# Ten late half modes fetched mode by mode, the mix-in one mode later, and the last 64 rows stored over three queues

## The chip, the cores and the metric

The kernel runs on one core of a Trainium2 chip. The metric is the device time of one execution in microseconds; each number given as "time" is a median over runs. A profile of one execution goes with it; its span runs from the first to the last instruction and is a little shorter than the time.

In this text PE or TensorE is the matrix engine, DVE or VectorE the vector engine, ACT or ScalarE the scalar engine, POOL or GpSimd the general engine, SP or sync the queue that only issues transfers. A q behind an engine's name means its instruction queue.

## The reference

Eight batches, eight heads, 576 positions, 64 channels per head. First a masked attention: heads 0 to 3 look at the last 32 positions, heads 4 to 7 at every 32nd position. The heads side by side are x (8 x 576 x 512). Then a spectral mix:

```python
X = np.fft.rfft(x, axis=1)
Y = np.zeros_like(X)
Xr, Xi = (np.real(X[:, :n_modes]), np.imag(X[:, :n_modes]))      # n_modes = 64
Yr = np.einsum('bmd,mde->bme', Xr, w_r) - np.einsum('bmd,mde->bme', Xi, w_i)
Yi = np.einsum('bmd,mde->bme', Xr, w_i) + np.einsum('bmd,mde->bme', Xi, w_r)
Y[:, :n_modes] = Yr + 1j * Yi
y = np.fft.irfft(Y, n=S, axis=1)
u = x + y
return (u + np.maximum(u @ w_ch, 0.0)).astype(np.float32)
```

Each of the 64 modes has a complex 512 x 512 matrix of its own, `w_r[m]` and `w_i[m]`, in 32-bit floats: 2 x 64 MB that have to be read once. All else is small beside it.

## The kernel before

**Weights.** A mode's matrix is split into two halves of 256 rows (a "half mode"); the list `ORDER` says in which sequence the 128 half modes are read. Its last 24 entries are half 1 of modes 56 to 63 and then half 0 of modes 48 to 63. `w_fetch` fetches two half modes, m and m + 1, into one tile `wt`: real parts on partitions 0 to 63, imaginary parts on 64 to 127. Normally that is one transfer for the real and one for the imaginary part of both modes, 512 KB each as 16-bit floats in the tile (the transfer converts). From entry 124 on (`i < 2 * NM - 4`), it is one transfer for each mode and part, 256 KB, sorted by mode: real and imaginary of m, then of m + 1. All are issued by GpSimd, in order. The tiles come from a pool of five (`NWBUF`), and a new fetch is asked for after the second mode of a pair has been multiplied.

**The order of the work.** The program is written out by hand, engine by engine in the order of the Python loops. While the weights stream in, the attention is computed, then its spectrum, then the modes are multiplied as they come: `mode(0, m)` for half 1 (pairs, line 597) and `mode(1, m)` for half 0 with m from 48 on (one mode at a time, line 630, 16 small products into one PSUM bank of eight modes). `spectrum` on VectorE (line 563) adds a group of modes to the tile `YT`. For the last group this is done twice: for modes 56 to 61 right after mode 61, and for modes 62 and 63 after mode 63.

**The late loop.** Its 24 steps are `rest`: steps 0 to 7 are half 1 of modes 56 to 63, steps 8 to 23 are half 0 of modes 48 to 63. Behind the products of step i come the functions in `late[i]`. Most are `renew(b, ts)`: it takes two tiles of 128 rows of batch b, adds what modes 0 to 47 contribute through the inverse transform to u @ w_ch (matmuls at lines 956 and 760, result copied by ScalarE) and to u (line 760, added by VectorE at line 961). `renew(b, (4,))` does it for the last 64 rows of two batches, a "half tile". At step 22 stand `v_early` (line 987) and `u_early` (line 992), which start the first two output items in PSUM.

**The tail.** After the last mode, `spec_z(3, 0)` (line 736) multiplies the last 16 modes of batches 0 to 3 by `w_ch`, and 18 output items follow: 16 of 2 batches x 128 rows, then two of 4 batches x 64 rows. For each, `new_rows` (line 1001) adds the last modes, `v_done` (line 1013, ScalarE) takes the positive part, and `u_done` (line 1020, VectorE) adds it to u and stores it: from the sync queue at line 1028 for the first 16 items, at line 1031 for the 64-row items, from the scalar queue for odd batches and from sync for even ones. The program closes at line 1108 with a drain on each engine and a barrier.

Of the kernel before, what the change touches and what calls it, by code (L numbers as in the profile page):

```python
# [19 lines left out]
NM = 64  # L20
# [36 lines left out]
def kernel(  # L57
# [10 lines left out]
    nc = tc.nc  # L68
# [17 lines left out]
    def psum(kind, half=False, pair=False):  # L86
        if pair:
            return pss[kind].tile([128, 2, 512], FP, tag=kind, name=kind)
        if half:
            return pss[kind].tile([128, 1024], F16, tag=kind, name=kind)  # L90
        return pss[kind].tile([128, 512], FP, tag=kind, name=kind)
# [65 lines left out]
    def w_fetch(n=1):  # L157
        for _ in range(n):
            i = len(w_tiles)
            if i >= 2 * NM:  # L160
                return
            half, m = ORDER[i]
            if i // 2 in GUEST:
                wt = big.tile([128, 2, 4, DM], F16, tag=GUEST[i // 2], name="wt")
            else:
                wt = pw.tile([128, 2, 4, DM], F16, tag="w", name="wt")
            single = []
            for ri, src in enumerate((moe_w_r, moe_w_i)):
                dst = wt[ds(64 * ri, 64)]
                rows = src[m : m + 2, ds(256 * half, 256), :].rearrange(  # L170
                    "m (p c) e -> p m (c e)", c=4
                )
                dst = dst.rearrange("p m c e -> p m (c e)")


                ones = range(2)
                if ri and not m:
                    ones = [1]
                elif i in UNEVEN and not ri:
                    a = 0  # L180
                    for n in UNEVEN[i]:
                        nc.gpsimd.dma_start(dst[a : a + n], rows[a : a + n])
                        a += n
                    continue
                elif i < 2 * NM - 4:
                    nc.gpsimd.dma_start(dst, rows)  # L186
                    continue
                single += [(j, ri, dst[:, j], rows[:, j]) for j in ones]
            for _, _, to, rows in sorted(single, key=lambda x: x[:2]):
                nc.gpsimd.dma_start(to, rows)  # L190
            w_tiles.extend((wt[:, 0], wt[:, 1]))
# [393 lines left out]
    def mode_pair(slot, m):  # L585
        half = 1 - slot
        if m % 4 == 0:
            ypt[slot] = psum("y")
        yp = ypt[slot]
        steps = [(c, mm) for c in range(4) for mm in (m, m + 1)]  # L590
        if m == 0:
            steps.sort(key=lambda x: x[1])
        for c, mm in steps:
            wt = w_tiles[ORDER.index((half, mm))]
            pr = ds(0, 128 if mm else 64)
            a = 32 * (mm % 4)
            nc.tensor.matmul(  # L597
                yp[ds(a, 32), :],
                Xh[half][pr, c].rearrange("p b r (h m) -> p (b r h) m", h=2)[
                    :, :, mm % 32  # L600
                ],
                wt[pr, XC[c], :],
                start=(c == 0),
                stop=(c == 3),
                tile_position=(0, a),
            )
        if slot or m // 2 not in GUEST:
            w_fetch()
        if m % 4:
            yr = big.tile([128, DM], F16, tag="yr", name="yr")  # L610
            act_copy(yr, yp)
            queued.append(lambda: four_turned(slot, m - 2, yr))

    def mode(slot, m):
# [22 lines left out]
        if m % 2:  # L637
            w_fetch()
# [131 lines left out]
    strided_tokens()  # L770
    load_str(2, 2)
    w_fetch()

    def str_front(b):
# [66 lines left out]
    for b in range(B):  # L841
# [12 lines left out]
        n = 0  # L854
        nm = NMODES[b]
        for mi in range(nm):
# [3 lines left out]
            n = upto  # L860
# [66 lines left out]
    n = 0  # L927
    for m in range(SPLIT0):
# [4 lines left out]
        n = upto  # L933
# [7 lines left out]
    def spec_late(mm, kept, eng):  # L941
        up = psum("p", pair=True)
        for bq in range(2):
            mm(2, bq, up[:, bq])
        for b in range(B):
            eng(kept[b][64:96], up[ds(32 * (b % 4), 32), b // 4])

    def renew(b, ts):
        n = len(ts)
        if n == 2:  # L950
            v0, xo = v0s[b][:, ts[0] : ts[0] + 2], xos[b][:, ts[0] : ts[0] + 2]
        else:
            v0, xo = v0h[b // 2].unsqueeze(1), xoh[b // 2].unsqueeze(1)
        vp, up = psum("p", pair=True), psum("p", pair=True)
        for j, t in enumerate(ts):
            nc.tensor.matmul(vp[:, j], idn, v0[:, j], start=True, stop=False)
            rows_of(b, t, vp[:, j], zzs, False)
        act_copy(v0, vp[:, 0:n])
        for j, t in enumerate(ts):
            rows_of(b, t, up[:, j], yys, True)  # L960
        nc.vector.tensor_tensor(out=xo, in0=up[:, 0:n], in1=xo, op=AluOp.add)  # L961
# [2 lines left out]
        spec_late(spec_y, yys, lambda o, i: nc.vector.tensor_copy(out=o, in_=i))  # L964

    late = {0: [lambda: spec_late(spec_z, zzs, act_copy)], 1: [spec_last]}
    for n, i in enumerate([3, 5, 7] + list(range(8, 21))):
        b, t = n // 2, n % 2 * 2
        late[i] = [lambda b=b, t=t: renew(b, (t, t + 1))]
        if n % 4 == 3:  # L970
            late.setdefault(i + (b == B - 1), []).append(lambda b=b: renew(b, (4,)))
# [5 lines left out]
    LAST = len(items) - 1  # L977
    vps, ups, rls, osbs = {}, {}, {}, {}

    def own(item, kept, half):  # L980
        bs, t = item
        return [kept[b][:, t] for b in bs] if t < 4 else [half[b // 2] for b in bs[::2]]

    def v_early(k):
        vps[k] = psum("p", pair=True)
        for j, r in enumerate(own(items[k], v0s, v0h)):
            nc.tensor.matmul(vps[k][:, j], idn, r, start=True, stop=False)  # L987

    def u_early(k):
        ups[k] = psum(("p", "u")[k % 2], pair=True)  # L990
        for j, r in enumerate(own(items[k], xos, xoh)):
            nc.tensor.matmul(ups[k][:, j], idn, r, start=True, stop=False)
# [12 lines left out]
    def pieces(k):  # L1005
        return [slice(0, 1), slice(1, 2)] if k == 0 else [slice(0, 2)]
# [8 lines left out]
    def u_done(k):  # L1015
        bs, t = items[k]
        up, rl = ups.pop(k), rls.pop(k)
        osb = pw.tile([128, 2, DM], FP, tag="w", name="osb")
        for j in pieces(k):
            nc.vector.tensor_tensor(  # L1020
                out=osb[:, j], in0=up[:, j], in1=rl[:, j], op=AluOp.add
            )
            if t < 4:
                rows = out[:, ds(128 * (t - t % 2), 256), :].rearrange(
                    "b (p i) e -> p b i e", i=2
                )
                own_b = slice(bs[0] + j.start, bs[0] + j.stop)
                nc.sync.dma_start(rows[:, own_b, t % 2], osb[:, j])
        if t == 4:
            for b in bs:  # L1030
                (nc.scalar if b % 2 else nc.sync).dma_start(
                    out[b, ds(512, 64), :], osb[ds(64 * (b % 2), 64), b // 2 % 2, :]
                )

    flush()
    rest = [(0, m) for m in range(SPLIT1, NM)] + [(1, m) for m in range(SPLIT0, NM)]
    late[22] = [lambda: v_early(0), lambda: v_early(1), lambda: u_early(0)]
    for i, (slot, m) in enumerate(rest):
        mode(slot, m)
        for w in late.get(i, ()):  # L1040
# [19 lines left out]
    for k in range(2):  # L1060
        if k:
            u_early(k)
        new_rows(k, ups[k], yys)
        u_done(k)
    for k in range(2, LAST + 2):
        if k == 8:
            held = psum("p", pair=True)[:, 0]
            spec_z(3, 1, held)
            act_copy(zzs[1], held)
        if k <= LAST:  # L1070
            v_early(k)
        if k > 2:
            u_early(k - 1)
        if k <= LAST:
            new_rows(k, vps[k], zzs)
        if k > 2:
            new_rows(k - 1, ups[k - 1], yys)
        if k <= LAST:
            v_done(k)
        if k > 2:  # L1080
            u_done(k - 1)
# [31 lines left out]
```

The softmax here doesn't subtract the row's maximum and nothing guards it: scores larger than these inputs give would overflow.

## Time and profile before

| what | value |
|---|---|
| time, median of 3 | 427.74 us (427.74 to 428.25) |
| span of the profile | 426.7 us |
| TensorE busy | 346.4 us (81%) |
| VectorE, ScalarE busy | 234.7 us (55%), 218.3 us (51%) |
| transfers on the GpSimd queue | 81.28 MB into the chip's memory, 96.2% of the 16 DMA engines' span |
| rate in slices 2 to 36 of the 40 equal slices of the span | 210 to 215 GB/s |
| stores of the last 64 rows | 4 from sync, 4 from scalar, 128 KB each, first issue 420.2 us, last 422.3 us |

The rate counts bytes as they arrive, and the weights arrive at half their size, so about twice as much is read from memory. Lines such as `PE L630` name an engine and a line of the kernel; `y<-X,wt` is what is written and what is read; `<-DMA wt...` behind a bracket says what ended the idle time before.

### The profile page before, as it was taken

Reading aid. Unit: us, or ns where it says so; the run is one execution under the profiler, and the core shown is the slowest. Engines: PE = TensorE matmul, PEld = TensorE weight load, DVE = VectorE, ACT = ScalarE, POOL = GpSimd, SP = SyncE. Lnnn points to the kernel's source line nnn. Section 1 sums busy time; section 2 is a strip of 40 time slices with the busy share of each in tenths; the row PEclk is TensorE's granted clock in tenths of the full one; section 3 lists DMA queues with packets and bytes.
Section 4 is the critical chain, followed back from the end, with each engine's and each line's share of the span. In section 5 each row is a group of like instructions: output and inputs, shape, how many; then the busy total and the mean of one; then the engine's idle time right before and its main releaser. Section 6 shows DMA issues by size and latency. Waiting matters only on the chain.

```text
span 426.7 us, 9768 instructions
## 1 busy us (share of the span) xinstructions
PE 346.4 (81%) x4167; PEld 208.2 (49%) x4167; DVE 234.7 (55%) x466; ACT 218.3 (51%) x390; POOL 110.7 (26%) x196
## 2 busy tenths in 40 slices
PE   2977878769999698889768788878788867889993
PEld 2866767554656365566433344435444423445330
DVE  3788778851355154356113246746676354655884
ACT  1687678643656356556642235423442444443872
POOL 8332333322423222222222322222232222210000
PEclk9999899967999689999995889989999979989997
DMA  8999999999999999999999999999999999995698
GB/s 150 210 212 212 213 213 213 211 211 211 214 213 213 213 213 215 212 214 215 210 214 211 213 214 213 210 213 215 212 213 214 213 213 214 214 212 105 244 355 287
DMA packets 30938, 91.62 MB, mean 215 GB/s; under 512 B 4464, under 2 KB 5232, under 8 KB 30896
## 3 DMA queue, kind: packets, MB, share of 16 engines
q0 software_dynamic: 25168, 81.28, 96.2%
q1 hardware_dynamic: 4976, 9.13, 5.9%
q10 hardware_dynamic: 752, 0.61, 0.5%
q8 instruction: 32, 0.52, 0.5%
q14 instruction: 10, 0.08, 0.0%
HBM read 162.83 MB, written 9.44 MB: 404 GB/s over the span
## 4 chain that ended last, share of the span: by engine, by line
DMA 47%; PE 29%; DVE 14%; ACT 5%; issue 3%; DVEq 0%; POOL 0%; ACTq 0%; POOLq 0%
DMA wt<-in_moe_w_i_dram 38%; DMA wt<-in_moe_w_r_dram 7%; PE y L597 5%; DVE xb L241 3%; DVE kz L283 3%; PE p L987 2%; ACT X L251 2%; PE sc L532 2%; PE tp L413 2%; PE sc L459 1%; PE p L1001 1%; PE y L532 1%; PE p L760 1%; DVE yy L752 1%; DVE rec L240 1%
## 5 line engine op out<-in xcount | busy, mean ns | idle before, releaser
L597 PE MATMUL y<-wt,X 128*32 128x512 f16 (+1 forms) x448 | 70.9, 430 | 20.1 <-DMA wt<-in_moe_w_i_dram 20.1
L186 POOL DMA_DIRECT2D wt<-in_moe_w_r_dram x59 | 34.7, 588 | 126.4 <-PE y L597 56.3
L186 POOL DMA_DIRECT2D wt<-in_moe_w_i_dram x60 | 35.4, 590 | 68.3 <-DMA wt<-in_moe_w_i_dram 44.4
L597 PEld LDWEIGHTS <-X 128*32 128x32 f16 (+1 forms) x448 | 28.1, 140 | 39.4 <-DMA wt<-in_moe_w_i_dram 18.6
L727 DVE COPY xo<-tp 128x512 f16<-128x512 f16 x32 | 22.1, 691 | 36.8 <-PE tp L725 36.8
L726 ACT ACTIVATE v<-sc 128x512 f16<-128x512 f32 x32 | 19.1, 597 | 44.2 <-PE sc L717 44.2
L717 PE MATMUL sc<-w_cp,xT 128*128 128x512 f16 x128 | 36.9, 410 | 1.9 <-DVE xT L690 1.9
L489 ACT ACTIVATE PL<-sc 128x480 f16<-128x480 f32 (+1 forms) x48 | 27.0, 578 | 21.3 <-PE sc L475 21.0
L241 DVE TENSOR_TENSOR xb<-av,rec 90x256 f16<-90x256 f32 (+2 forms) x80 | 36.0, 450 | 2.8
L240 DVE RECIPROCAL rec<-av 90x4 f32<-90x4 f32 (+2 forms) x80 | 14.6, 183 | 39.3 <-PE av L504 28.2
L251 ACT ACTIVATE yr<-y 128x512 f16<-128x512 f32 x28 | 16.7, 597 | 36.8 <-PE y L597 35.6
L961 DVE TENSOR_TENSOR xo<-p,xo 128x1024 f16<-128x1024 f32 x16 | 19.6, 1225 | 21.7 <-PE p L760 21.7
L420 DVE COPY qT<-tp 128x576 f16<-128x576 f16 x16 | 11.9, 752 | 34.7 <-PE tp L413 34.7
L251 ACT ACTIVATE v<-p 128x1024 f16<-128x1024 f32 x16 | 16.4, 1023 | 23.1 <-PE p L760 23.1
L378 ACT ACTIVATE PL<-sc 90x360 f16<-90x360 f32 (+1 forms) x48 | 22.7, 490 | 7.0 <-PE sc L371 6.4
L251 ACT ACTIVATE v<-tp 128x640 f16<-128x640 f16 (+1 forms) x24 | 19.0, 807 | 11.8 <-PE tp L447 9.3
L413 PE MATMUL tp<-cI_s,ring 64*64 64x64 f16 x864 | 22.4, 197 | 2.7 <-DVE qT L420 2.4
L459 PE MATMUL sc<-cMl_s,cI_s 128*128 128x480 f16 (+1 forms) x48 | 19.4, 405 | 4.5 <-ACT PL L489 2.9
L276 PE MATMUL tp<-cI_s,ring 72*128 72x72 f16 x256 | 15.4, 207 | 8.7 <-DMA ring<-in_v_dram 7.1
L413 PEld LDWEIGHTS <-ring 64*64 64x64 f16 x864 | 17.5, 110 | 9.4 <-issue 5.4
L251 ACT ACTIVATE kz<-tp 64x360 f16<-64x360 f16 (+1 forms) x32 | 18.9, 592 | 6.2 <-PE tp L413 5.2
L1013 ACT ACTIVATE rl<-p 128x1024 f32<-128x1024 f32 (+1 forms) x19 | 18.4, 979 | 5.7 <-PE p L1001 3.1
(142 smaller groups left out, 737.9 us busy)
## 6 DMA issues: line engine op xcount, KB each, us to landing
wt<-in_moe_w_i_dram POOLq DMA_DIRECT2D x60, 512.0 KB, 18.8
wt<-in_moe_w_r_dram POOLq DMA_DIRECT2D x59, 512.0 KB, 17.7
out_dram<-osb SPq DMA_DIRECT2D x15, 512.0 KB, 3.4
ring<-in_v_dram POOLq DMA_DIRECT2D x8, 288.0 KB, 13.4
ring<-in_q_dram POOLq DMA_DIRECT2D x8, 288.0 KB, 13.6
ring<-in_k_dram POOLq DMA_DIRECT2D x8, 288.0 KB, 13.1
ring<-in_v_dram POOLq DMA_DIRECT2D x3, 512.0 KB, 14.8
ring<-in_q_dram POOLq DMA_DIRECT2D x3, 512.0 KB, 14.8
```

The costliest lines, as they stand in the source:

```text
L186: nc.gpsimd.dma_start(dst, rows)
L241: nc.vector.tensor_tensor(out=dst, in0=val.rearrange("p h (q c) -> p h c q", c=4), in1=rec[0:n, 0:pieces] .to_broadcast((n, pieces, 64)) . ...
L251: nc.scalar.activation(out=out, in_=in_, func=ACTF.Copy)
L378: nc.scalar.activation(out=PS[0:n, ds(POFF[t], 4 * n)], in_=scp[0:n, 0 : 4 * n], func=ACTF.Exp, scale=SCALE,)
L413: nc.tensor.transpose(tp[ds(64 * hp, 64), ds(64 * i, 64)], qn[ds(64 * hp, 64), ds(64 * (9 * g + i), 64)], idn[ds(64 * hp, 64), ds(64 * hp, ...
L459: nc.tensor.matmul(scp[:, 0 : n * times].rearrange("p (h x) -> p h x", h=times), idn, mask_rows("cMl", n, times), start=True, stop=False,)
L489: nc.scalar.activation(out=dst, in_=src, func=ACTF.Exp, scale=SCALE)
L597: nc.tensor.matmul(yp[ds(a, 32), :], Xh[half][pr, c].rearrange("p b r (h m) -> p (b r h) m", h=2)[:, :, mm % 32], wt[pr, XC[c], :], start= ...
L717: nc.tensor.matmul(vp, xT[:, ch], w_chs["cp"][:, ch, :], start=(ch == 0), stop=(ch == 3),)
L726: nc.scalar.activation(out=v0, in_=vp, func=ACTF.Copy)
L727: nc.vector.tensor_copy(out=xo.rearrange("p (h q c) -> p h q c", h=2, c=4), in_=tp[:, 0:512].rearrange("p (h c q) -> p h q c", h=2, c=4),)
L961: nc.vector.tensor_tensor(out=xo, in0=up[:, 0:n], in1=xo, op=AluOp.add)
```

## The change

Three edits. Five more pairs of half modes (modes 50 to 59 of half 0) are fetched mode by mode, so that the first mode of a pair can be multiplied before the second has come. The mix-in `renew` stands one mode step later from the third on; `u_early` moves behind the last mode. And the stores of the last 64 rows are issued from three queues (sync, scalar, GpSimd) in place of two, to shorten the row of issues at the end.

```diff
-                elif i < 2 * NM - 4:
+                elif i < 2 * NM - 14:
                     nc.gpsimd.dma_start(dst, rows)
                     continue
                 single += [(j, ri, dst[:, j], rows[:, j]) for j in ones]
...
-    for n, i in enumerate([3, 5, 7] + list(range(8, 21))):
+    for n, i in enumerate([3, 5] + list(range(8, 22))):
         b, t = n // 2, n % 2 * 2
         late[i] = [lambda b=b, t=t: renew(b, (t, t + 1))]
...
         if t == 4:
+            q = [nc.sync, nc.scalar, nc.gpsimd, nc.scalar if k == LAST else nc.gpsimd]
             for b in bs:
-                (nc.scalar if b % 2 else nc.sync).dma_start(
+                q[b % 4].dma_start(
                     out[b, ds(512, 64), :], osb[ds(64 * (b % 2), 64), b // 2 % 2, :]
                 )
...
-    late[22] = [lambda: v_early(0), lambda: v_early(1), lambda: u_early(0)]
+    late[22] += [lambda: v_early(0), lambda: v_early(1)]
+    late[23] = [lambda: u_early(0)]
```

With it, `renew` of the last batch's second pair of tiles falls to step 21 (mode 61) and its half tile to step 22, ahead of the two `v_early`. Of the first 64-row item (batches 0 to 3) sync and scalar store one batch each and GpSimd two; of the last one (batches 4 to 7) sync stores one, scalar two and GpSimd one.

## The prediction

> **What bounds the kernel now.** I read the page's slices first, then the chain of waits, then each late weight transfer's issue and landing, then the order of the tensor engine's work around the end of the stream, and last the end of the program. The queues and the chain come from the page:
>
> ```profile
> q0 software_dynamic: 25168, 81.28, 96.2%
> ...
> DMA 47%; PE 29%; DVE 14%; ACT 5%; issue 3%; DVEq 0%; POOL 0%; ACTq 0%; POOLq 0%
> ```
>
> The queue filled by GpSimd keeps 16 DMA engines at work for 96% of the span: the weights are the bound, until they have landed. The chain in order of time shows the hand-over:
>
> ```profile
> 357.73 19.38 DMA wt<-in_moe_w_i_dram
> 377.10 0.14 issue
> 377.24 0.64 PE y L630 x16
> ...
> 389.94 0.56 DVE YT L563
> 390.50 0.04 issue
> 390.54 0.64 PE y L630 x16
> ...
> 393.33 1.05 PE zp L736 x4
> ...
> 419.83 1.44 DVEq L1108
> ```
>
> From 377.24 on the chain runs over TensorE alone, and from 393.33 (`spec_z` on the last spectrum) over the tail of output items. So two questions decide: how much earlier can 393.33 be, and how soon after the last addition is the program over.
>
> For the first, the view of the weight tile, one transfer at a time. The last one:
>
> ```profile
> L190 POOL DMA_DIRECT2D wt<-in_moe_w_i_dram x1: 515/515/515, 382.3 to 382.3; - x1
> ...
> DMA to landing us min/median/max: 9.6/9.6/9.6
> ```
>
> 382.31 + 9.6 = 391.9 is the landing of mode 63's imaginary half. The same view gives, for the single transfers before it, 383.3, 384.5, 385.7, 387.0, 388.2, 389.5 and 390.7: one every 1.23 us. The pairs land at 367.3 (modes 52/53), 372.2 (54/55), 377.1 (56/57) and 382.1 (58/59), so 2.45 us for each transfer of twice the size. Per byte they are equal. The timeline of TensorE beside that:
>
> ```profile
> 377.24 0.64 PE L630 MATMUL y<-X,wt 128*128 128x16 f16 x16 [1.24 <-DMA wt<-in_moe_w_i_dram]
> ...
> 390.54 0.64 PE L630 MATMUL y<-X,wt 128*128 128x16 f16 x16 [0.53 <-DVE YT L563]
> 391.01 1.02 PE L987 MATMUL p<-v,cI_s 128*128 128x512 f16 x4
> 391.87 0.59 PE L992 MATMUL p<-xo,cI_s 128*128 128x512 f16 x2
> 392.31 0.64 PE L630 MATMUL y<-X,wt 128*128 128x16 f16 x16
> 393.33 1.04 PE L736 MATMUL zp<-w_ch,YT 128*128 128x512 f16 x4 [0.39 <-DVE YT L563]
> ```
>
> Mode 63 starts at 392.31, only 0.4 us after its weights are there. That 0.4 us is all that any reordering of TensorE can win, unless the stream itself ends sooner.
>
> For the second, the view of the line where the program ends:
>
> ```profile
> L1108 SPq EVENT_SEMAPHORE  x11: 17/28/28, 422.7 to 426.6; - x11
> L1108 POOLq EVENT_SEMAPHORE  x4: 17/17/17, 425.9 to 426.6; - x4
> L1108 POOLq DRAIN  x3: 51/98/12676, 382.3 to 426.4; - x3
> ```
>
> GpSimd's first drain starts with its last DMA (382.3) and takes 12.68 us: to 394.98. Its descriptor work was over at 382.31 + 0.52 = 382.83, so the drain waited for the transfers, and ended 3.1 us after the last of them landed (391.9). Today nobody notices: GpSimd isn't needed again until the closing barrier at 425.9.
>
> **What the Trainium skill says.** "DMA: Bandwidth & Descriptors", section "Issuing engines are not separate DMA queues": transfers started from several engines share the same 16 DMA engines, and starting them on several only saves issue time. The trace agrees: in the stretches of 1 us from 421 to 424 the DMA share is already 0.94, 0.97 and 0.95. Same page, "Latency and other measured facts": the first byte of a transfer from GpSimd takes about 1 us, from sync or scalar about 0.6 us; no store here leaves from GpSimd, so the trace doesn't show it for one. "Perfetto Trace Analysis", "DMA Instruction — SWDGE (GPSIMD)": the profiled bar ends when the descriptors are written, not when data has moved; the 0.52 us bar against the landing after 9.6 us agrees. "TensorE: Matmul & The Clock Gate", Part 1: after an idle window of about 3.4 us the clock halves. The trace has it at 378 to 380 (granted 0.50; a 128x512 matmul every 0.43 us instead of 0.22). I found no page that says what a drain on GpSimd waits for.
>
> **The change, part by part.** *Single transfers for modes 50 to 59.* Five pairs of 2 x 512 KB become 20 of 256 KB, 10 more issues. Each is 0.52 us on GpSimd, which idles about 1.9 us before each late issue: hidden. In the trace eight transfers are open at a time (when mode 63's last is issued at 382.31, the one eight before it has just landed at 382.1). Eight singles are 8 x 1.23 = 9.8 us of stream. The last eight of today run on that depth already, still at 1.23 us each, so I expect no loss. The stream's end stays at 391.9, give or take 0.4. What changes is that the first mode of each pair may start 2.45 us earlier: landings every 2.45 us, 372.2 (55), 374.7 (56), 377.1, 379.6, 382.1, 384.5, 387.0 (61), 389.5 (62), 391.9 (63).
>
> *Mix-in one mode later.* A mode (0.49 us) with one `renew` (1.29 us) takes 1.78 us, as between 386.81 and 388.60 - less than the 2.45 us of its weights; with the half tile too, 2.97 us (370.39 - 367.42). From mode 48 at 357.58 TensorE falls behind at first. The `renew` at mode step 7 is gone, so it idles from about 354 to 357.6, and may run the next 3.4 us at half clock: some 1.7 us. It catches up by 0.67 us a mode and is level with the stream at mode 60 (384.6). Then: mode 61 at 387.1, done with its `renew` at 388.9; mode 62 at 389.6. Its spectrum of six modes on VectorE is queued ahead of the last big addition and done near 388.2, so the 0.53 us wait goes. After mode 62 come 0.49 + 1.18 (half tile of the last batches) + 0.86 (`v_early` twice) = 2.53 us, to 392.15: mode 63 starts there instead of at 392.31. `u_early(0)`, 0.43 us, now lies behind mode 63, in the 0.54 us in which TensorE waits for VectorE's last spectrum: hidden. Gain on this path: 0.16 us; bounds 0.4 (all the slack) and -0.4 (stream later, or half clock at the end).
>
> *The tail* from 393.3 to the last addition's end at 420.06 + 1.22 = 421.28 isn't touched: ends at 421.12.
>
> *Stores of the last 64 rows.* Now 4 issues on sync and 4 on scalar, 0.56 to 0.58 us each, the last at 422.3 landing 3.3 us later, at 425.6; then 1.1 us to the end. After: of the last item one store on sync, two on scalar, one on GpSimd. Scalar's second starts at about 421.8 and lands at 425.1: 0.5 us earlier on that side. The GpSimd store is issued at 421.2. From issue to landing I bound it below by the 3.3 us of the other queues and above by the first load of the trace from GpSimd, 5.0 us for twice the bytes; I take 3.7, so 424.9. What stands behind it on GpSimd is the drain, and the barrier waits for that. Its excess over the landing is 3.1 us in the only case this trace has, which I take: 428.0. Lower bound 0 (if a short drain sees its one transfer at once), upper 5 us. From GpSimd's first barrier event to the end is 426.7 - 425.9 = 0.8: span 428.8.
>
> Sum: 428.8 - 426.7 = +2.1 us; 427.74 + 2.1 = **429.8 us**.
>
> **The rivals.** *A: the drain costs nothing.* Then the end hangs on the scalar queue: 425.1 + 1.1 = 426.2, 0.5 us sooner, 427.2 us. For it: the page's chain never names GpSimd's drain, and one drain over eight queued loads need not price one after a single store. Against: 12.68 us can't be a drain's own cost when the two others took 0.10 and 0.05.
> *B: faster, because the stream ends sooner.* From 388 to 391.5 the DMA share falls from 0.86 to 0.08: some engines lag. If smaller transfers even them out, mode 63 could start up to 1.5 us earlier if its queue on TensorE is shortened as well, and with a free drain the time is about 426.2. Against: that tail already consists of single transfers, and TensorE has 2.5 us of work between modes 62 and 63.
> *C: a shallower queue starves the stream.* If 9.8 us in flight isn't enough for the lagging engine, the ten modes cost perhaps 0.1 us each: 1 us more, 430.8 with the drain. Against: today's last eight singles.
> *D: the drain is dearer,* 5 us: 431.7.
>
> **How the numbers follow.** Drain as computed 0.52, C 0.06, D 0.06, A 0.20, B 0.16. The first three are slower by over 0.2% (0.86 us): 0.64. A is within it: 0.20. B is faster: 0.16. The range reaches from just under A, 427.0, to D, 431.7; it leaves out B and the worst of D and C.
>
> **What would show it.** Right: GpSimd's long drain begins near 421.2 and ends after 427, about 3 us behind its last store, and the closing events follow it; mode 63 starts within 0.4 us of 392.15; single landings stay at 1.23 us; the last addition ends near 421. Wrong: the first closing event of GpSimd follows sync's last by 0.1 us as today, or the last weight lands more than 1 us off 391.9.

## The result, and the profile after

The changed kernel takes 432.17 us (median of 4 runs, 431.53 to 434.46) against 427.74 us: ratio 1.0108, 95% interval 1.0089 to 1.0128. The prediction had the direction and the cause, a drain on GpSimd at the end, but at 429.8 us less than half of the size, and the time lies 0.5 us above its range.

The page of the changed kernel, queues and chain:

```profile
q0 software_dynamic: 25472, 81.67, 95.9%
...
DMA 48%; PE 21%; DVE 4%; issue 2%; ACT 2%; POOL 1%; POOLq 0%; DVEq 0%; ACTq 0%
```

The weights still fill 96% of the span. POOL has come into the chain with 1%, a small share with much behind it. The chain's last pieces in order of time (start, length, what):

```profile
418.12 1.24 DVE osb L1020
419.36 0.28 issue
419.64 0.47 POOL out_dram L1032
...
420.75 0.55 POOLq L1110
```

The chain's last piece begins at 420.75 on GpSimd and is followed only to 421.3, in a span of 429.8 us. What comes next is in the view of the program's last line (here L1110; count, shortest, median and longest in ns, first and last start):

```profile
L1110 SPq EVENT_SEMAPHORE  x11: 17/28/28, 422.6 to 429.7; - x11
L1110 POOLq EVENT_SEMAPHORE  x4: 17/17/17, 429.0 to 429.7; - x4
L1110 POOLq DRAIN  x3: 51/97/8218, 420.8 to 429.5; - x3
...
L1110 SPq DRAIN  x3: 7/7/7, 426.0 to 429.2; - x3
```

The long drain of GpSimd now starts at 420.75 and takes 8.22 us, to 428.97. Sync is through with its waits at 426.0, as before at 425.8; GpSimd's first closing event comes at 429.0, when the drain is over. Three microseconds lie between. The last store from GpSimd, in the view of the store line:

```profile
L1032 POOL DMA_DIRECT2D out_dram<-osb x1: 529/529/529, 420.8 to 420.8; - x1
...
DMA to landing us min/median/max: 4.6/4.6/4.6
```

It landed at 420.76 + 4.6 = 425.4, so the drain outlasted it by 3.6 us.

And the end of the weight stream, in TensorE's timeline of the changed kernel:

```profile
356.77 0.64 PE L630 MATMUL y<-X,wt 128*128 128x16 f16 x16 [3.52 <-DMA wt<-in_moe_w_i_dram]
...
386.50 0.64 PE L630 MATMUL y<-X,wt 128*128 128x16 f16 x16 [0.51 <-DMA wt<-in_moe_w_i_dram]
...
389.21 0.64 PE L630 MATMUL y<-X,wt 128*128 128x16 f16 x16 [0.76 <-DMA wt<-in_moe_w_i_dram]
...
391.52 0.64 PE L630 MATMUL y<-X,wt 128*128 128x16 f16 x16
391.99 0.59 PE L992 MATMUL p<-xo,cI_s 128*128 128x512 f16 x2
392.54 1.04 PE L736 MATMUL zp<-w_ch,YT 128*128 128x512 f16 x4
```

The last weights land at 391.3 (issued 381.68, 9.6 us), and mode 63 starts at 391.52, 0.8 us sooner than in the profile of before. That looks like a gain and is none: mode 48, whose weights no edit touches, already starts at 356.77 against 357.58. From there to mode 63 it is 34.75 us now and 34.73 before; from mode 63 to the end of the last addition (420.49) it is 28.97 us in both. From mode 48 on the two profiles differ in one stretch alone: from the last addition to the end it is 9.3 us against 5.4.

### The profile page after: what moved, and what is told of

Read it like the earlier page. It is cut to its first block, busy times and chain, and to the rows that moved or that the text cites. A ratio compares the mean times of both kernels' runs of the same rounds, so it can differ in the third digit from the quotient of the medians.

```text
span 429.8 us, 9787 instructions
## 1 busy us (share of the span) xinstructions
PE 340.9 (79%) x4167; PEld 206.4 (48%) x4167; DVE 235.1 (55%) x466; ACT 218.3 (51%) x390; POOL 117.0 (27%) x209
## 4 chain that ended last, share of the span: by engine, by line
DMA 48%; PE 21%; DVE 4%; issue 2%; ACT 2%; POOL 1%; POOLq 0%; DVEq 0%; ACTq 0%
DMA wt<-in_moe_w_i_dram 31%; DMA wt<-in_moe_w_r_dram 13%; PE y L597 5%; DMA ring<-in_v_dram 4%; PE sc L717 3%; PE p L987 2%; PE p L1001 1%; DVE yy L752 1%; PE p L992 1%; PE y L532 1%; PE tp L725 1%; ACT X L251 1%; PE u L992 1%; PE tp L413 1%; PE sc L459 1%
## 5 line engine op out<-in xcount | busy, mean ns | idle before, releaser
L597 PE MATMUL y<-wt,X 128*32 128x512 f16 (+1 forms) x448 | 67.6, 413 | 22.5 <-DMA wt<-in_moe_w_i_dram 22.4
L186 POOL DMA_DIRECT2D wt<-in_moe_w_r_dram x54 | 31.8, 589 | 110.2 <-PE y L597 35.7
L186 POOL DMA_DIRECT2D wt<-in_moe_w_i_dram x55 | 32.6, 592 | 64.3 <-DMA wt<-in_moe_w_i_dram 40.1
```

What stands on the lines that cost most here:

```text
L597: nc.tensor.matmul(yp[ds(a, 32), :], Xh[half][pr, c].rearrange("p b r (h m) -> p (b r h) m", h=2)[:, :, mm % 32], wt[pr, XC[c], :], start= ...
```

## The experiments

The kernel before was timed again with each group of experiments, at 427.86 to 427.99 us, and each ratio below is against its own group.

**1. Stores back on two queues.**

```diff
-            q = [nc.sync, nc.scalar, nc.gpsimd, nc.scalar if k == LAST else nc.gpsimd]
-                q[b % 4].dma_start(
+                (nc.scalar if b % 2 else nc.sync).dma_start(
```

> The changed kernel with the stores of the last 64 rows on two queues as before; single transfers and the later mix-in stay. Theory S (the store edit costs everything; the other two edits are worth nothing): 427.7 us, within 0.5 of before, and from mode 48's start to mode 63's start 34.7 us as in both kernels. Rival W (the single transfers or the later mix-in cost part of it): 428.5 us or more. Rival G (they gain what the profile seems to show, the last addition 0.8 us earlier): 426.9.

428.32 us (13 runs), ratio 1.0013 (0.9998 to 1.0029). In the profile mode 48 starts at 356.72, mode 63 at 391.52, the last addition ends at 420.49 and the span at 426.0. The time alone, 0.46 us above before with an interval that takes in 1, would not settle rival W; but the median span of these runs is 426.2 us and that of before's 426.1, so within the span the other two edits neither gain nor cost. The store edit carries almost everything; rival G falls.

**2. The store edit alone,** on the kernel before (the same two lines as in the change).

> The kernel before with only the store edit. Theory S: 431.6 to 432.2 us; last addition to end 9.3 us against 5.4 before; GpSimd's drain ends 3 to 4 us after its last store has landed, and the closing events follow at once. Rival W: less than 430.5.

431.64 us, ratio 1.0085 (1.0070 to 1.0101). Last addition to end: 430.1 - 421.1 = 9.0 us. Its own drain, and GpSimd's closing event behind it:

```profile
L1109 POOLq EVENT_SEMAPHORE  x4: 17/17/17, 429.4 to 430.0; - x4
L1109 POOLq DRAIN  x3: 51/98/7976, 421.4 to 429.9; - x3
```

The long drain runs from 421.36 for 7.98 us, to 429.3, and the closing event follows at 429.4. The store edit alone makes 3.8 of the 4.4 us of loss.

**3. No GpSimd store in the last item.**

```diff
-            q = [nc.sync, nc.scalar, nc.gpsimd, nc.scalar if k == LAST else nc.gpsimd]
+            q = [nc.sync, nc.scalar] * 2 if k == LAST else [nc.sync, nc.scalar, nc.gpsimd, nc.gpsimd]
```

> The changed kernel with GpSimd storing only batches 2 and 3 of the first 64-row item; the last item on sync and scalar. Theory S with a drain of landing plus a fixed excess of 3.1 to 3.6 us: GpSimd's last store is issued 0.57 us sooner and so the end comes about 0.6 to 1.0 us sooner, 431.2 us. Rival N (the excess grows with the number of open transfers, 3 then and 2 now): 1.5 us or more sooner, 430.5. Rival L (only a store behind the last addition matters): 427.7.

The profile ends 1.0 us sooner (428.8; median span of the runs 429.0 against 429.95), the drain at 420.11 + 7.90 = 428.01, 3.5 us behind its last landing (420.2 + 4.3). That is theory S with the same excess for two transfers as for three. The time is 431.74 us, ratio 1.0090 (1.0069 to 1.0110), hardly below the changed kernel's: two of four runs have 0.8 to 1.6 us more outside the span than the usual 1.8 (see the last section). Rival L falls in any case.

**4. One early store from GpSimd,** on the kernel before.

```diff
-                nc.sync.dma_start(rows[:, own_b, t % 2], osb[:, j])
+                (nc.gpsimd if k == 8 else nc.sync).dma_start(rows[:, own_b, t % 2], osb[:, j])
```

> The kernel before with one 512 KB store, that of item 8, some 11 us ahead of the last addition, issued from GpSimd. Theory S with a drain of landing plus 3.1 to 3.6 us: the drain is over long before the end, 427.7 us, and its end minus the landing gives the excess for a single transfer, 3.1 to 3.6 us. Rival F (any store from GpSimd has a fixed price at the end): 429 us or more. Rival N (excess grows with open transfers): same time, but an excess near 1 us.

428.33 us, ratio 1.0014 (1.0006 to 1.0022): 0.5 us, not 4. The drain, in the view of its last line:

```profile
L1108 POOLq DRAIN  x3: 51/98/6885, 408.5 to 425.9; - x3
```

It ends at 408.5 + 6.9 = 415.4, long before the end, and 3.6 us behind the landing of its one transfer (408.52 + 3.3 = 411.8). So neither a store from GpSimd as such nor the number of open transfers sets the price of 4 us: rivals F and N fall. The trace has the other 0.5 us elsewhere. Up to the store's issue the DMA share matches that of before, microsecond by microsecond; then, between 409 and 410, it is 0.40, where the stretches of 1 us on either side and the one of before at this place have 1.02 to 1.04: the engines ran dry for some 0.6 us before this store's bytes moved. Until the last addition they stay near 1, so the gap isn't made up: from the last addition to the end it is 5.9 us in place of 5.4.

**5. One GpSimd store in all,** that of batch 6 in the last item.

```diff
-            q = [nc.sync, nc.scalar, nc.gpsimd, nc.scalar if k == LAST else nc.gpsimd]
+            q = [nc.sync, nc.scalar, nc.gpsimd if k == LAST else nc.sync, nc.scalar]
```

> The changed kernel with one GpSimd store only, of batch 6 in the last item, the other seven on sync and scalar. Theory S (the end is the landing of GpSimd's last store plus a fixed 3.1 to 3.6 us plus 0.85): issued at once behind the last addition, it lands 3.3 to 4.5 us later; span 428.3 to 429.5, time 430.3 to 431.3. Rival N (the excess shrinks with one transfer): under 429.5.

431.17 us, ratio 1.0071 (1.0056 to 1.0087). Issued 0.3 us behind the last addition, landed after 3.5 us, at 425.5; the drain ended at 421.96 + 7.49 = 429.45, 4.0 us later. With the other two edits still in, one transfer of 128 KB on GpSimd is enough for 3.2 us of the 4.4.

Together the drains of eight profiles (experiments 10 and 11 are told below; the excess is worked out before rounding, which makes 3.0 us of the prediction's 3.1):

| kernel | last transfers from GpSimd | last landing | drain ended | excess |
|---|---|---|---|---|
| before | 8 loads | 391.9 | 395.0 | 3.0 |
| changed | 3 stores | 425.4 | 429.0 | 3.6 |
| store edit alone | 3 stores | 426.2 | 429.3 | 3.2 |
| none in the last item | 2 stores | 424.5 | 428.0 | 3.5 |
| one in the last item | 1 store | 425.5 | 429.5 | 4.0 |
| one early | 1 store | 411.8 | 415.4 | 3.6 |
| changed, 64-row items in the middle (10) | 4 stores | 415.4 | 419.2 | 3.8 |
| before, 64-row items in the middle (11) | 4 stores | 415.5 | 418.7 | 3.2 |

A drain of fixed length, whatever the transfers do, does not fit: it took 12.7 us over loads that landed 9.6 us after their issue, and 6.9 to 8.2 us over stores that landed after 3.3 to 4.8.

**6. The single transfers alone** (the first line of the change).

> The kernel before with only the five more pairs fetched mode by mode. Theory S: the stretch from mode 48's start to mode 63's start stays at 34.7 us and the time within 0.5 us of before. Rival C (a shallower queue starves the stream): the stretch grows by 1 us or more.

428.28 us, ratio 1.0012 (1.0001 to 1.0023); mode 48 to mode 63 34.6 us (357.17 to 391.80). No gain, a loss of some 0.4 us (0.0 to 1.0 by the interval), and no starved stream: the last single transfer is issued 1.24 us behind the one before it (380.84, 382.08), the pace of before.

**7. The later mix-in alone** (the `late` lines of the change).

> The kernel before with only the mix-in one mode later and the last start of an item behind mode 63. Theory S: without the single transfers TensorE catches up less, mode 63 starts up to 0.5 us later than with pairs in the old place; the time within 0.7 us of before, 428.2. Rival H (the later mix-in alone is the gain that was meant): 427.2 or less.

427.95 us, ratio 1.0002 (0.9994 to 1.0011); the stretch is 35.2 us in its profile. Nothing in the time.

**8. Half as many issues.** If issuing were what the end waits for, fewer issues would help without GpSimd.

```diff
-            for b in bs:
-                (nc.scalar if b % 2 else nc.sync).dma_start(
-                    out[b, ds(512, 64), :], osb[ds(64 * (b % 2), 64), b // 2 % 2, :]
+            for h in range(2):
+                (nc.scalar if h else nc.sync).dma_start(
+                    out[bs[0] + h : bs[0] + 4 : 2, ds(512, 64), :].rearrange("b p e -> p b e"),
+                    osb[ds(64 * h, 64), :, :],
                 )
```

> The kernel before with the stores of the last 64 rows merged: for each item one transfer of 256 KB for the even batches on sync and one for the odd on scalar, so that each queue issues two in place of four and none is on GpSimd. Theory S: the last issue comes about 0.6 us sooner than before's (at once behind the last addition) and the end 0.3 to 0.7 us sooner: 427.3 us. Rival E (the 16 engines are already full, so issue time is worth nothing): 427.8, no difference.

428.66 us, ratio 1.0015 (1.0007 to 1.0023), slower. The last issues begin at 421.0, at once behind the last addition (420.97), and land up to 4.7 us later, where before the last of four began at 422.3 and landed 3.3 us later. Theory S was wrong on this: earlier issues bought nothing. Rival E has the better reason, full engines, but it expected no difference: from 421 to 423 the merged stores moved 182 and 215 GB/s, the single ones of before 244 and 334. Why larger transfers are slower here is not shown.

That also bears on the change. The last addition ends at 420.49 in the kernel with two queues (experiment 1) and in the changed one. Busy time by stretches of 1 us of the kernel with two queues (length; busy us and instructions of PE, PEld, DVE, ACT, POOL; granted clock, DMA share, GB/s):

```profile
419.50:420.50 1.00, 0.00 (x0) 0.00 (x0) 0.99 (x1) 0.00 (x0) 0.00 (x0) 1.00 1.00 379
420.50:421.50 1.00, 0.00 (x0) 0.00 (x0) 0.00 (x0) 0.00 (x0) 0.00 (x0) 1.00 0.99 258
421.50:422.50 1.00, 0.00 (x0) 0.00 (x0) 0.00 (x0) 0.00 (x0) 0.00 (x0) 0.80 0.92 316
```

And the changed kernel, in the same view:

```profile
419.50:420.50 1.00, 0.00 (x0) 0.00 (x0) 0.98 (x1) 0.00 (x0) 0.86 (x2) 1.00 0.99 375
420.50:421.50 1.00, 0.00 (x0) 0.00 (x0) 0.00 (x0) 0.00 (x0) 0.76 (x2) 1.00 1.05 219
421.50:422.50 1.00, 0.00 (x0) 0.00 (x0) 0.00 (x0) 0.00 (x0) 0.00 (x0) 1.00 0.92 246
```

The DMA share is near 1 in both: there was no idle DMA time that a third queue could fill. With it the engines move less, 219 and 246 against 258 and 316 GB/s, and every store of the last item lands later: 4.5 to 4.7 us after its issue, those from sync and scalar too, against 3.0 to 3.4. The last item needs no GpSimd store for that: in experiment 3, where GpSimd stores two batches of the item before and none of the last, the last item's stores landed after 4.3 to 4.6 us. Even without the drain the third queue would have lost something: sync, which waits for all stores, is through with its waits at 426.0 in the changed kernel and at 425.1 in experiment 1. Why the engines move less is not settled.

**9. and 10. The 64-row items in the middle.** If slow stores and the drain hurt because they stand last, they can stand elsewhere.

```diff
     for P0 in (0, 2):
         items += [((2 * P, 2 * P + 1), t) for t in range(4) for P in (P0, P0 + 1)]
-    items += [(range(b, b + 4), 4) for b in (0, 4)]
+        items += [(range(b, b + 4), 4) for b in (0, 4)][:2 - P0]
```

> The kernel before with the two 64-row items moved from places 16 and 17 to places 8 and 9, so that the last item is one of 128 rows with a single 512 KB store from sync. Theory O: what follows the last addition shrinks from 5.4 us to the issue-to-landing of such a store, 3.3 us, plus 1.1: 4.5 us, so 0.9 us sooner, 427.0. Rival E (the bytes through the 16 engines set the end, whatever their order): 427.9, no difference.

> The whole changed kernel, its four stores from GpSimd included, with the same reordering: GpSimd's last store then leaves some 10 us ahead of the last addition. Theory S (only the landing of GpSimd's last transfer plus 3.1 to 4.0 us of drain counts): the drain ends before the last store of sync has landed, the penalty is gone, 427.0 to 428.3. Rival F (stores from GpSimd cost several us wherever they stand): 430 or more.

The changed kernel with this order (10): 429.57 us, ratio 1.0041 (1.0023 to 1.0060), where in its own order it stands at 1.0108. Same edits, same four GpSimd stores (one more than in the change, since no item of 64 rows is last any more); only their place differs. The drain runs from 411.4 for 7.8 us and is over at 419.2, while the last addition is still ahead:

```profile
L1110 POOLq DRAIN  x3: 51/98/7802, 411.4 to 426.8; - x3
```

So 2.6 of the 4.4 us go with the place. The time is above what was expected, for three reasons: the order has a price of its own (9, below); from the last addition to the end it is 5.7 us in place of 4.7 in 9, sync's last store landing after 4.3 us in place of 3.7, so the GpSimd stores seem still to cost transfer time; and some executions have up to 1.2 us more outside the span than usual. Against 9 that is 1.1 us and not several, so rival F falls.

The kernel before with this order (9): 428.50 us, ratio 1.0012 (1.0004 to 1.0019). The end did shrink as theory O had it, from 5.4 to 427.1 - 422.4 = 4.7 us. It was given back at a new wait, which VectorE's timeline has (in brackets the idle time before, and what ended it):

```profile
409.85 1.23 DVE L1020 TENSOR_TENSOR osb<-u,rl 128x1024 f32<-128x1024 f32 x1 [0.40 <-PE u L1001]
412.07 1.23 DVE L1020 TENSOR_TENSOR osb<-p,rl 128x1024 f32<-128x1024 f32 x1 [1.00 <-ACT rl L1013]
```

and its chain names what stood in front of ScalarE's work:

```profile
409.47 0.56 ACTq L1031
410.07 0.83 ACTq L1031
411.01 1.03 ACT rl L1013
```

The stores on the scalar queue hold ScalarE up for 1.4 us of issue in front of the next positive part. At the end of the program nothing was behind them.

**11. and 12. The same order with scalar free.**

In 11:

```diff
-                (nc.scalar if b % 2 else nc.sync).dma_start(
+                (nc.gpsimd if b % 2 else nc.sync).dma_start(
```

> The two 64-row items at places 8 and 9 as in the reordering, their odd batches stored from GpSimd in place of scalar, so that no issue stands in front of ScalarE's next positive part. Theory O2 (the reordering lost its gain to scalar's issues in front of the next item, 1.0 to 1.4 us): last addition 1.0 us or more sooner after mode 63 than in the reordering, 30.4 to 29.4 us or less, the drain over near 419, time 427.3. Rival E (the bytes of the stores are the bound): 428.3 as in the reordering.

In 12:

```diff
-                (nc.scalar if b % 2 else nc.sync).dma_start(
+                nc.sync.dma_start(
```

> The same with all eight stores of the 64-row items on sync. Theory O2: ScalarE is free of issues, but sync has 8 x 0.57 us to issue in the time of two items, so later stores leave some 1 to 2 us late and catch up at 0.37 us each; last addition as in the GpSimd variant, time 427.5. Rival E: 428.3.

11: 429.12 us, ratio 1.0036 (1.0023 to 1.0049). 12: 430.10 us, ratio 1.0056 (1.0043 to 1.0069). Theory O2 was right on the wait and wrong on the time. In 11 the last addition ends 29.3 us after mode 63's start, in 12 29.8, not 30.4 as in 9, yet the program isn't over sooner. Busy time by stretches of 2 us in 11 says why:

```profile
410.00:412.00 2.00, 2.00 (x15) 0.59 (x14) 1.90 (x2) 1.15 (x2) 1.46 (x3) 1.00 0.89 250
412.00:414.00 2.00, 2.00 (x12) 0.64 (x12) 1.86 (x3) 1.70 (x2) 0.07 (x1) 1.00 0.91 277
...
418.00:420.00 2.00, 1.39 (x9) 0.39 (x8) 1.93 (x3) 1.26 (x2) 0.00 (x0) 1.00 1.03 384
420.00:422.00 2.00, 0.00 (x0) 0.00 (x0) 0.96 (x1) 0.00 (x0) 0.00 (x0) 1.00 1.03 379
422.00:424.00 2.00, 0.00 (x0) 0.00 (x0) 0.00 (x0) 0.00 (x0) 0.00 (x0) 0.83 1.04 385
424.00:426.00 2.00, 0.00 (x0) 0.00 (x0) 0.00 (x0) 0.00 (x0) 0.00 (x0) 0.50 0.47 174
```

While the 64-row stores leave, the engines move 250 to 277 GB/s; after that they run full at about 380 to the last byte, 3.9 us beyond the last addition. In 12, with no store from GpSimd, it is 192 and 199 GB/s from 410 to 414, then again about 380, and the program ends 6.6 us behind the last addition. The stores that are slow in the middle leave a backlog for the end here. That is rival E's mechanism, the bytes, with a larger loss than it expected. No version of these twelve beats the kernel before.

## Why the prediction was wrong, point by point

- *Direction and cause:* right. GpSimd's drain begins behind its last store, outlasts it by some 3 us, and the closing events wait for it. Experiments 2 to 5 and 10 show it: what matters most is how near the end GpSimd's last transfer stands.
- *The size* is where it failed: the step "Stores of the last 64 rows". Predicted from the last addition (421.12) to the end (428.8): 7.7 us; measured 9.3. Three terms of that sum were too small. The issue: 0.08 us behind the last addition was assumed, 0.27 measured (420.76 against 420.49). GpSimd's two stores of the item before need not be the reason: in experiment 5 nothing stood in front and it was 0.3 us too, and the first GpSimd store after the change began 0.28 us behind its addition (419.36 to 419.64). The landing: 3.7 us taken, 4.6 measured. It was priced by transfers of the kernel before, where no store leaves from GpSimd; with GpSimd stores in the item before, all stores of the last item are late (experiment 3, and the rates under experiment 8), without them GpSimd's landed after 3.5 us (experiment 5). Why is open. The excess of the drain: 3.1 taken from its single case, 3.6 measured, 3.0 to 4.0 over eight profiles. 0.2 + 0.9 + 0.5 = 1.6 us, all in one direction.
- *The stream and the mix-in:* a gain of 0.16 us was forecast, none came (34.75 against 34.73 us), within the bounds of 0.4 either way. Single profiles can't tell so little: this stretch is 34.4 to 34.9 us in the seven without these two edits and 34.7 to 35.2 in the five with both. One sign named in advance failed: mode 63 starts at 391.52, not within 0.4 us of 392.15, since in that execution the stream was 0.8 us early from mode 48 on. Most pieces were right: no starving, level with the stream before mode 61, VectorE's 0.53 us wait gone, and `u_early` hidden: mode 63 to `spec_z` is 1.02 us with it as without it. As foreseen, the slack of mode 63 was too small to matter. The reading of the chain was a little too simple: its own lines have VectorE in it at 389.94.
- *The clock:* TensorE ran at half clock as foreseen (128x512 matmuls every 0.43 us from 357.6 to 362), but not for the reason given. The granted clock is 0.50 already at 353, before the idle time of 3.52 us that ends at 356.77. And in the profile of before, the halving at 378 to 380 that the prediction cites as agreement follows a wait of 1.24 us, while one of 2.02 us (357.58) is followed by none. So these traces don't bear out that an idle window of about 3.4 us is what halves the clock; what does stays open.
- *The rest:* of the 2.4 us between 429.8 and 432.17, the stores are 1.6 and the gain that did not come 0.2. Some 0.4 us show in no profile: with both other edits in, part of the executions spend more time outside the span. The prediction had no term for that.
- *Rival A* (a free drain, stores 0.5 us sooner) was wrong twice: the drain isn't free, and the stores land later, not sooner (experiments 1, 8 and the rates there). Rival B: the stream ended no sooner, 34.5 us from mode 48's start to the last landing against 34.4. Rival C: single landings stayed 1.23 us apart on average. Rival D had the right side of the error and too little of it.
- *The range* failed because each unknown cost was bounded alone but only the drain's upper end was put into it; the landing's upper bound of 5.0 us, close to the truth, was left out of D.

## What to carry to other kernels

Look at what each engine has to do after its last instruction before giving it one more: a drain that nobody waits for becomes the end of the program when that engine gets the last transfer. Here a third queue brought the last issue forward from 421.51 (experiment 1) to 421.06, and with a DMA share near 1 that was worth nothing; ask for the bytes and their rate first. Before two profiles are compared at their end, line them up at a point that no edit touches: here that turned a seeming gain of 0.8 us into none.

## What the runs showed that was not expected

The drain's excess over the landing, 3.0 to 4.0 us, was about the same for loads and stores, for stores of 128 KB and of 512 KB, and for one open transfer as for eight. What it does in that time stays open.

At the end of the program, in stretches of 1 us with a DMA share over 0.8, stores of 64 rows moved at about 180 to 340 GB/s and the stores of 128 rows ahead of them at 360 to 395. The share alone doesn't tell how many bytes move.

Time less span is 1.7 to 2.1 us in all 115 executions of the kernel before that were timed with the experiments, and with the single transfers or the later mix-in alone. With both it was 2.5 to 3.4 us in about every third execution (4 of 13 in experiment 1, 2 of 4 in the changed kernel and in experiment 3, 4 of 9 in experiment 10; none of 4 in experiment 5). No profile shows that time, and its cause wasn't found.
